# Spectral layer and MLP on one core: the fourth sequence's first stage as stacked products, and split loads in the passage to the MLP

## The chip, the cores and the metric

The kernel runs on one core of a Trainium2 chip. Its engines work side by side, each on its own queue in order: TensorE (PE, with its weight loads PEld), VectorE (DVE), ScalarE (ACT), GpSimd (POOL) and SyncE (SP), which here only starts transfers. Times are microseconds on the device, and the number that counts is the median of several runs.

## What is computed

Four sequences of 3008 tokens with 256 channels go through a spectral layer (a real Fourier transform over the tokens, a complex 256x256 product with bias, a soft threshold, the inverse transform) and then through an MLP with 2048 hidden channels.

```python
X = np.fft.rfft(x, axis=1)                       # x: (4, 3008, 256)
Yr = X.real @ w_r - X.imag @ w_i + b_r
Yi = X.real @ w_i + X.imag @ w_r + b_i
Yr, Yi = (np.sign(v) * np.maximum(np.abs(v) - 0.01, 0.0) for v in (Yr, Yi))
y = np.fft.irfft(Yr + 1j * Yi, n=3008, axis=1).reshape(12032, 256)
h = y @ moe_w_in                                 # 256 -> 2048
out = (h / (1 + np.exp(-h))) @ moe_w_out         # 2048 -> 256
```

## The kernel before

The transform is split as 3008 = 47 x 64. The first stage (`s1`) is a product over the 47, done for two halves of the 64 at once: 94 rows of x against a table with 96 columns, in eight pieces per sequence of 1024 columns each, one piece in two halves of 512. Its result goes through a scratch in DRAM. `s2_3` is the second forward stage, `mix3` the complex product, its deferred part the threshold, `split_z` and `i1` the first inverse stage, which stores into a second scratch; `i2` is the last inverse stage, which makes the columns `xt` of one block of 512 tokens for the MLP.

For precision, products of 32-bit numbers are made of high and low parts in a rounded 32-bit format (`F32R`): a value is cast on ScalarE, the difference is taken on VectorE, and three matmuls (high with high, high with low, low with high) stand for one. In the fourth sequence's first stage `s1_split` does the cast (L215) and the difference (L216) for one half, `s1_half` the three matmuls (L173) and the copy of the result (L226).

The order of the work is written by hand. After a prologue (the first sequence's spectral part, most of the second's first stage), the MLP runs in 384 ticks. Tick t does, in this order on every engine's queue: `split_g` of the tick before (L512, L513), the threshold left over from a mix product, `mlp1` of tick t (six matmuls at L495, then sigmoid and product on ScalarE and VectorE), the work that `fill` lists for tick t, a few stores, and `mlp2` of tick t - 2 (L535, L539). `put` finds for a piece of spectral work the next tick that is not in `taken`. The MLP weights come as 64-bit numbers and are turned into high and low parts in three steps of two VectorE instructions each, beside ScalarE casts; `w_go` does steps, and `W_GO` says how many in tick 0, 1, 2, and so on.

The passage from prologue to MLP stands at L734 to L755: the last two `u_step`, `s1` for pieces 2 to 5 of the second sequence, the loads of the first MLP block (`i2_load(0)`, two transfers at L409 of 96 rows from the second scratch), `i2` of block 0 with the two halves of piece 6 between (`s1_later`), the load for block 1. Piece 7 follows in the ticks.

Of the kernel before, what the change touches and what calls it, by code (L numbers as in the profile page):

```python
# [19 lines left out]
RR, KK = 47, 64  # L20
# [9 lines left out]
W_GO = [2, 1, 1, 2, 1, 1, 2, 1, 0, 0, 0, 2, 1, 2, 1, 2, 1, 2, 1, 1, 2, 1, 2, 1]  # L30

S1_SPLIT = (3, 4, 5, 6, 7)

# [4 lines left out]
def dft_tables():  # L38
# [16 lines left out]
    for h in range(2):  # L55
# [34 lines left out]
    c3f = c3  # L90
    return {
# [4 lines left out]
        "c3f": c3f,  # L96
    }
# [3 lines left out]
def spectral_mlp_kernel(ctx: ExitStack, tc: tile.TileContext, x, w_r, w_i, b_r, b_i, w_in, w_out, c1, c2, c3, c4, c3f, out):  # L101
# [9 lines left out]
    c4_sb = cst.tile([96, NP], F32, name="c4_sb")  # L111
    bias = cst.tile([128, 2, D], F32, name="bias")
# [48 lines left out]
    x_next = [(b, g) for b in range(NB) for g in range(8)]  # L161

    def x_ahead():
        if x_next:
            q = x_next.pop(0)
            x_t[q] = x_load(*q)
# [8 lines left out]
    def s1(b, g, late=False):  # L175
        t = x_t.pop((b, g))
        tag, bufs = ("s1o", 2) if 8 * b + g in (6, 7, 10, 11, 12, 13) else ("gin", 4)
        o = sb.tile([128, 4 * D], F32, tag=tag, bufs=bufs, name="s1o")[:96, :]
# [40 lines left out]
    def s1_half(b, g, i):  # L219
        sx = x_t.pop((b, g, i))  # L220
        if i == 0:
            x_t[b, g, "o"] = sb.tile([128, 4 * D], F32, tag="s1o", bufs=2, name="s1o")[:96, :]
        o = x_t[b, g, "o"]
        p = bank("s1")
        s1_product(p, (sx[:, 0, :], sx[:, 1, :]))
        nc.scalar.copy(o[:, i * 512:(i + 1) * 512], p[:96, :])  # L226
        if i == 0:
            s1_split(b, g, 1)
        else:
            v = scr1[b].rearrange("r (a j) d -> (r a) (j d)", a=4)  # L230
            store(v[:, g * 4 * D:(g + 1) * 4 * D], o)
            del x_t[b, g], x_t[b, g, "o"]
            x_ahead()

# [171 lines left out]
    def g_load(b, g):  # L406
        t = sb.tile([96, 4 * D], F32, tag="gin", bufs=4, name="gin")
        v = scr2[b].rearrange("r (a j) d -> (r a) (j d)", a=4)
        nc.sync.dma_start(out=t, in_=v[:, g * 4 * D:(g + 1) * 4 * D])  # L409
        g_t[b, g] = t  # L410
# [200 lines left out]
    with tc.manual_schedule():  # L611
# [123 lines left out]
        s1(1, 2, late=True)  # L735
        flush(1)
        u_step(NU + 1)
        s1(1, 3, late=True)
        i2_load(0)
        flush(1)  # L740
# [4 lines left out]
        flush(1)  # L745
# [40 lines left out]
        for i in range(2):  # L786
            put(2, s1_later, 7, i)
        for t in (11, 35):
            at(t, x_ahead)
        m3 = mix3_weights()  # L790
# [10 lines left out]
        for b, t0, dt in ((2, 37, 6), (3, 110, 8)):  # L801
# [49 lines left out]
```

## Time and profile before

| | us |
|---|---|
| median of 3 runs | 1383.81 (1381.85 to 1385.62) |
| profiled execution | 1383.51 |
| its span in the trace | 1381.5 |
| TensorE busy | 1363.3 |
| VectorE busy | 888.2 |
| ScalarE busy | 705.5 |
| GpSimd busy | 98.8 |

A group of instructions is named by the line of the kernel, the engine, the operation and the tiles it writes and reads. Matmuls overlap their neighbours, so the step from one start to the next is what one costs in a row. The granted clock (PEclk) is a share of TensorE's full 2.4 GHz; 0.50 is its lower level.

### The profile page before, as it was taken

The page shows a single profiled execution, that of the slowest core. Times are in us where ns is not written, and L with a number is a line of the kernel's source. Part 1 is how long each engine was busy: PE and PEld are TensorE (multiplying, and loading weights), DVE is VectorE, ACT ScalarE, POOL GpSimd, SP SyncE. Part 2 cuts the span into 40 slices and gives each one's busy share as a digit, 9 for nine tenths or more (in the row PEclk, how much of TensorE's full clock was granted, in tenths as well). Part 3 has the DMA queues.
Part 4 walks back from the last instruction along what each step waited for, and adds up shares of the span by engine and source line. Part 5 has one row for each costly group of instructions (what it writes and reads, how often), then busy time and mean ns, then how long its engine had stood idle before and what let it go on. Part 6 is the DMA issues. An engine that isn't in the chain of part 4 may idle for free.

```text
span 1381.5 us, 20358 instructions
## 1 busy us (share of the span) xinstructions
PE 1363.3 (99%) x7621; PEld 1168.3 (85%) x7621; DVE 888.2 (64%) x1517; ACT 705.5 (51%) x1386; POOL 98.8 (7%) x145
## 2 busy tenths in 40 slices
PE   8998999999999999999999999999999999999998
PEld 4976788888888888888888888888888888888888
DVE  3867979687655677767655577776654555455555
ACT  5445555555564555555454445454454444444444
POOL 2000012111000101111100011111000000000000
PEclk9999999999999999999999999999999999999999
DMA  8874334231423214333121022220210110011001
GB/s 263 268 226 144 93 88 119 76 97 32 123 76 101 58 43 107 89 94 81 50 73 54 20 77 60 75 81 25 61 32 12 27 39 10 18 27 39 0 16 24
DMA packets 69932, 103.51 MB, mean 75 GB/s; under 512 B 7306, under 2 KB 53002, under 8 KB 69834
## 3 DMA queue, kind: packets, MB, share of 16 engines
q1 hardware_dynamic: 58163, 79.07, 19.8%
q0 software_dynamic: 8096, 19.45, 5.4%
q10 hardware_dynamic: 3575, 3.70, 0.8%
q8 instruction: 60, 0.98, 0.3%
q14 instruction: 38, 0.31, 0.1%
HBM read 64.70 MB, written 37.49 MB: 74 GB/s over the span
## 4 chain that ended last, share of the span: by engine, by line
PE 94%; DMA 2%; DVE 2%; ACT 1%; issue 1%; SPq 0%; ACTq 0%; DVEq 0%
PE h L495 37%; PE acc L535 24%; PE acc L539 12%; PE mix L349 6%; PE i L438 3%; PE s L324 2%; PE mix L288 2%; PE s L173 2%; PE i L397 2%; PE s L189 1%; PE acc L530 1%; PE s L267 1%; PE i L394 1%; PE i2e L438 1%; DMA t3f<-in_c3f_dram 1%
## 5 line engine op out<-in xcount | busy, mean ns | idle before, releaser
L495 PE MATMUL h<-xt,win 128*128 128x512 f32 (+1 forms) x2304 | 585.5, 389 | 0.4 <-DVE g L503 0.2
L535 PE MATMUL acc<-wout,gh 128*128 128x512 f32 x1472 | 540.7, 401 | 0.0
L495 PEld LDWEIGHTS h<-xt,win 128*128 128x128 f32 x2304 | 401.7, 188 | 82.7 <-ACT xt L454 0.5
L502 ACT ACTIVATE g<-h 128x512 f32<-128x512 f32 (+1 forms) x385 | 226.1, 587 | 385.0 <-PE h L495 384.1
L503 DVE TENSOR_TENSOR g<-h,g 128x512 f32<-128x512 f32 (+1 forms) x385 | 261.0, 678 | 239.8 <-ACT g L502 236.5
L539 PE MATMUL acc<-wout,gl 128*128 128x256 f32 x1472 | 413.1, 281 | 1.3 <-DVE gl L513 1.3
L513 DVE TENSOR_TENSOR gl<-g,gh 128x512 fp32r<-128x512 f32 (+1 forms) x385 | 276.0, 717 | 169.2 <-ACT gh L512 165.0
L535 PEld LDWEIGHTS acc<-wout,gh 128*128 128x128 f32 x1472 | 277.6, 189 | 59.4 <-issue 0.5
L512 ACT CAST gh<-g 128x512 fp32r<-128x512 f32 (+1 forms) x385 | 235.3, 611 | 158.5 <-DVE g L503 155.9
L539 PEld LDWEIGHTS acc<-wout,gl 128*128 128x128 f32 x1472 | 278.6, 189 | 11.5 <-DVE gl L513 2.4
L356 POOL TENSOR_TENSOR q<-q,bias 128x256 f32<-128x256 f32 x36 | 26.4, 733 | 652.6 <-ACT q L355 652.6
L438 PEld LDWEIGHTS i<-c_sb,gin 96*128 96x128 f32 x420 | 54.9, 193 | 8.6 <-issue 4.3
L369 DVE TENSOR_TENSOR y<-q,mix 64x256 f32<-64x256 f32 x144 | 60.3, 419 | 2.2
L438 PE MATMUL i<-c_sb,gin 96*128 96x94 f32 x420 | 54.2, 274 | 3.3 <-DMA gin<-scr 3.3
L324 PEld LDWEIGHTS s<-t,a 128*128 128x128 f32 x288 | 37.7, 191 | 3.0
L324 PE MATMUL s<-t,a 128*128 128x128 f32 x288 | 37.9, 275 | 0.0
L455 DVE TENSOR_TENSOR xt<-i,xt 128x376 fp32r<-128x376 f32 (+2 forms) x48 | 28.0, 583 | 12.4 <-ACT xt L454 6.7
L173 PE MATMUL s<-sx,c 94*96 94x512 f32 (+1 forms) x111 | 34.1, 414 | 0.2 <-DVE sx L216 0.2
L397 PE MATMUL i<-zh,t 128*128 128x256 f32 x144 | 33.7, 297 | 0.0
L401 ACT COPY i1o<-i 128x512 f32<-128x512 f32 x48 | 27.8, 580 | 10.2 <-PE i L394 9.0
L556 DVE TENSOR_TENSOR o<-acc,o 128x256 f32<-128x256 f32 x92 | 32.6, 413 | 0.0
L357 POOL TENSOR_TENSOR q<-q,bias 128x256 f32<-128x256 f32 x36 | 31.9, 886 | 2.8
(118 smaller groups left out, 1164.7 us busy)
## 6 DMA issues: line engine op xcount, KB each, us to landing
a<-scr SPq DMA_DIRECT2D x48, 256.0 KB
gin<-scr SPq DMA_DIRECT2D x32, 384.0 KB
scr<-s1o SPq DMA_DIRECT2D x31, 384.0 KB
t<-in_c_dram POOLq DMA_DIRECT2D x36, 256.0 KB, 3.0
scr<-i1o SPq DMA_DIRECT2D x36, 256.0 KB
x_sb<-in_x_dram POOLq DMA_DIRECT2D x22, 376.0 KB, 4.1
t<-in_c_dram SPq DMA_DIRECT2D x48, 128.0 KB
w<-in_moe_w_in_dram SPq DMA_DIRECT2D x8, 512.0 KB
```

Source lines behind the costliest of these rows:

```text
L173: nc.tensor.matmul(out=p[:96, :], lhsT=c1_hl[m][:K, :], rhs=hl[k][:K, :], start=(n == 0), stop=(n == 2))
L324: nc.tensor.matmul(out=pv[:, e, :, r, :], lhsT=a[:, r, e * 128:(e + 1) * 128], rhs=t2[:, r * 128:(r + 1) * 128], start=True, stop=True,)
L349: nc.tensor.matmul(out=out, lhsT=x_[:, e, c, :], rhs=m[:, e, :], start=(n == 0), stop=(n == 5))
L397: nc.tensor.matmul(out=pv[:, r, :], lhsT=t3[:, m, q], rhs=z[k][:, r, :], start=(n == 0), stop=(n == 2),)
L438: nc.tensor.matmul(out=p[:, o:o + m], lhsT=g_t[b, j // 4][:, q:q + 128], rhs=c4_sb[:, p0:p0 + m], start=True, stop=True,)
L495: nc.tensor.matmul(out=p[:, :n], lhsT=w[:, e, f * 128:(f + 1) * 128], rhs=v[:, e, :n], start=(m == 0), stop=(m == 5),)
L502: nc.scalar.activation(out=g[:, q], in_=p[:, q], func=ACTF.Sigmoid)
L503: nc.vector.tensor_tensor(out=g[:, q], in0=p[:, q], in1=g[:, q], op=ALU.mult)
L512: nc.scalar.copy(gh[:, q], g[:, q])
L513: nc.vector.tensor_sub(gl[:, q], g[:, q], gh[:, q])
L535: nc.tensor.matmul(out=a, lhsT=gh[:, q], rhs=wout[:, f].rearrange("p a c -> p (a c)"), start=begins, stop=False,)
L539: nc.tensor.matmul(out=a[:, D:2 * D], lhsT=gl[:, q], rhs=wout[:, f, 0, :], start=False, stop=ends,)
```

## The change

Three things change.

The fourth sequence's first stage is done in sixteen pieces instead of eight, with the two halves of the 64 in separate pieces. A piece has 47 rows of x, and these are loaded twice, to rows 0 to 46 and 64 to 110 of one buffer; rows 32 to 63 are set to zero once for each of the two buffers. `stack_split` casts all 111 rows, and takes the difference in rows 64 to 110, so that high and low parts lie one above the other. The new table `c5` holds the table's high part in 48 columns and its low part in 48 others (from column 64), and both again for the lower rows. One matmul per 512 columns gives (high + low) times the high part in PSUM rows 0 to 47 and (high + low) times the low part in rows 64 to 111; these are copied out by ScalarE and added by VectorE.

In the passage the two loads of the first MLP block are each cut in two: 88 rows after the next to last inverse store, and the last 8 rows after the last one. The results of pieces 4 and 5 go to x buffers that are no longer in use, the two halves of piece 7 move to later ticks, and stores are started in another order.

`W_GO` has other numbers: 13 steps instead of 11 in ticks 0 to 7, and 17 instead of 19 from tick 11 on.

```diff
-W_GO = [2, 1, 1, 2, 1, 1, 2, 1, 0, 0, 0, 2, 1, 2, 1, 2, 1, 2, 1, 1, 2, 1, 2, 1]
+W_GO = [2, 2, 1, 2, 1, 2, 2, 1, 0, 0, 0, 2, 1, 2, 1, 2, 1, 2, 1, 2, 1, 1, 1]
+STACKED = 3
...
+    def x_load_twice(b, q):
+        t = x_sb[q % 2]
+        if b == STACKED and q < 2:
+            nc.gpsimd.memset(t[32:64, :], 0.0)
+        h, g = divmod(q, 8)
+        v = x[b].rearrange("(n h j) d -> n h (j d)", h=2, j=NJ)[:, h, g * 4 * D:(g + 1) * 4 * D]
+        for p in (0, 64):
+            nc.gpsimd.dma_start(out=t[p:p + RR, :], in_=v)
+        return t
...
-        tag, bufs = ("s1o", 2) if 8 * b + g in (6, 7, 10, 11, 12, 13) else ("gin", 4)
-        o = sb.tile([128, 4 * D], F32, tag=tag, bufs=bufs, name="s1o")[:96, :]
+        if b == 1 and g in (4, 5):
+            o = x_pre[g + 1][:96, :]
+        else:
+            tag, bufs = ("s1o", 2) if 8 * b + g in (6, 7, 10, 11) else ("gin", 4)
+            o = sb.tile([128, 4 * D], F32, tag=tag, bufs=bufs, name="s1o")[:96, :]
...
+    def stack_split(b, q):
+        t = x_t[b, q]
+        sx = sb.tile([128, 4 * D], F32R, tag="sx", bufs=1, name="sx")
+        nc.scalar.copy(sx[:64 + RR, :], t[:64 + RR, :])
+        nc.vector.tensor_sub(sx[64:64 + RR, :], t[64:64 + RR, :], sx[64:64 + RR, :])
+        x_t[b, q] = sx
+
+    def stack_product(b, q):
+        sx = x_t.pop((b, q))
+        o = sb.tile([128, 4 * D], F32, tag="s1o", bufs=2, name="s1o")[:2 * NR, :]
+        for i in range(2):
+            p = bank("s1")
+            c = slice(i * 512, (i + 1) * 512)
+            nc.tensor.matmul(out=p, lhsT=c5_sb[:64 + RR, :], rhs=sx[:64 + RR, c], start=True, stop=True)
+            nc.scalar.copy(o[:, c], p[64:64 + 2 * NR, :])
+            nc.vector.tensor_tensor(out=o[:, c], in0=p[:2 * NR, :], in1=o[:, c], op=ALU.add)
+        h, g = divmod(q, 8)
+        v = scr1[b].rearrange("r (i h j) d -> (r i) h (j d)", i=2, h=2)
+        store(v[:, h, g * 4 * D:(g + 1) * 4 * D], o)
+        x_ahead()
...
         u_step(NU)
         s1(1, 2, late=True)
+        for g in range(2):
+            loaded.add((0, g))
+            g_load(0, g, slice(0, 88))
         flush(1)
         u_step(NU + 1)
         s1(1, 3, late=True)
-        i2_load(0)
-        flush(1)
+        for g in range(2):
+            g_load(0, g, slice(88, 96))
         s1(1, 4, late=True)
         w_go()
         w_tags[:] = [(("zl", 2), ("zh", 2))]
         s1(1, 5, late=True)
-        flush(1)
+        flush(2)
...
-            put(2, s1_later, 7, i)
+            put(5, s1_later, 7, i)
...
+        at(30, nc.gpsimd.dma_start, c5_sb, c5)
...
-        for b, t0, dt in ((2, 37, 6), (3, 110, 8)):
+        t = 0
+        for q in range(16):
+            t = max(t, int(110 + 4.4 * q))
+            at(t, stack_split, 3, q)
+            t = put(t + 1, stack_product, 3, q)
+        for b, t0, dt in ((2, 37, 6),):
```

The changed kernel is longer, so its lines have other numbers: L409 becomes L461, L142 becomes L157, L579 becomes L630, L495, L535 and L539 become L546, L586 and L590, and L205 becomes L234.

On SyncE, in the passage, this stood in the row before: the store of piece 2 of the second sequence, the two loads of block 0, then stores and a weight load (`scr` with `s1o` is a store of the first stage, `gin` a block's load, `w` a weight load).

```order
L142 DMA scr_1_83<-s1o 96x1024
L409 DMA gin<-scr_0_86 96x1024 x2
L142 DMA scr_1_83<-s1o 96x1024
L579 DMA w_999<-in_moe_w_out_dram 128x2x512
L142 DMA scr_1_83<-s1o 96x1024
L409 DMA gin<-scr_0_86 96x1024
L142 DMA scr_1_83<-s1o 96x1024
L579 DMA w_1055<-in_moe_w_in_dram 128x1024
```

And now, at the same place on SyncE:

```order
L461 DMA gin<-scr_0_87 88x1024 x2
L157 DMA scr_1_84<-s1o 96x1024
L461 DMA gin<-scr_0_87 8x1024 x2
L630 DMA w_1000<-in_moe_w_out_dram 128x2x512
L157 DMA scr_1_84<-s1o 96x1024
L157 DMA scr_1_84<-x_pre 96x1024
L461 DMA gin<-scr_0_87 96x1024
L157 DMA scr_1_84<-x_pre 96x1024
L630 DMA w_1056<-in_moe_w_in_dram 128x1024
```

The long parts of the loads now stand ahead of the store of piece 2, the short parts behind it, and the stores of pieces 3 and 4 follow the weight load together.

On TensorE, tick 2 had the end of `mlp1`, the first half of piece 7 and the start of `mlp2` in this row before (`h` is `mlp1`, `s` the first stage, `acc` is `mlp2`):

```order
L495 MATMUL h<-xt_1013,win_79 128x512
L495 MATMUL h<-xt_1013,win_80 128x512
L495 MATMUL h<-xt_1014,win_79 128x512
L205 MATMUL s_1123<-x_sb_69,c_sb 96x512
L535 MATMUL acc<-wout,gh 128x512
L539 MATMUL acc<-wout,gl 128x256
```

And now, in tick 2 on TensorE:

```order
L546 MATMUL h<-xt_1014,win_80 128x512
L546 MATMUL h<-xt_1014,win_81 128x512
L546 MATMUL h<-xt_1015,win_80 128x512
L586 MATMUL acc<-wout,gh 128x512
L590 MATMUL acc<-wout,gl 128x256
```

The half of piece 7 is gone from here, and `mlp2` follows `mlp1` directly; the two halves stand in ticks 6 and 7.

On VectorE, ticks 132 and 133 (a step of the third sequence, then no spectral product) read like this before (`xs`, `xl` belong to the second stage, `zl` to the inverse, `g` and `gl` to the MLP):

```order
L334 TENSOR_TENSOR xs<-s_6008,xs 128x256
L336 TENSOR_TENSOR xl<-s_6008,xh 128x2x256
L337 TENSOR_TENSOR xl<-xs,xh 128x2x128
L383 TENSOR_TENSOR zl<-y,zh 128x512
L513 TENSOR_TENSOR gl<-g,gh 128x512
L503 TENSOR_TENSOR g<-h,g 128x512
L513 TENSOR_TENSOR gl<-g,gh 128x512
```

And now, in the same two ticks on VectorE:

```order
L384 TENSOR_TENSOR xs<-s_6033,xs 128x256
L386 TENSOR_TENSOR xl<-s_6033,xh 128x2x256
L387 TENSOR_TENSOR xl<-xs,xh 128x2x128
L433 TENSOR_TENSOR zl<-y,zh 128x512
L268 TENSOR_TENSOR sx<-x_sb_70,sx 47x1024
L564 TENSOR_TENSOR gl<-g,gh 128x512
L554 TENSOR_TENSOR g<-h,g 128x512
L279 TENSOR_TENSOR s1o<-s_6088,s1o 48x512
L279 TENSOR_TENSOR s1o<-s_6092,s1o 48x512
L564 TENSOR_TENSOR gl<-g,gh 128x512
```

The difference of a stacked piece now stands behind that step and ahead of the tick's `gl`, and the two additions of its product stand behind the next tick's `g`.

## Rows read from the trace of the kernel before

**Rows 1.** The page, busy time: engine, us, share of the span, instructions.
```profile
PE 1363.3 (99%) x7621; PEld 1168.3 (85%) x7621; DVE 888.2 (64%) x1517; ACT 705.5 (51%) x1386; POOL 98.8 (7%) x145
```

**Rows 2.** Waits of PE: line waited for, us in total, times, longest.
```profile
PE s L205 <- DMA x_sb<-in_x_dram: 3.7, 1, 3.7
```

**Rows 3.** Chain of waits, 88 to 120 us: start us, us, what.
```profile
90.62 2.89 DMA scr<-i1o
...
93.57 4.43 DMA gin<-scr
```

**Rows 4.** Stretches: us, then busy us (instructions) of each engine, clock, DMA share, GB/s.
```profile
core 0: us, PE busy (x) PEld busy (x) DVE busy (x) ACT busy (x) POOL busy (x), PEclk, DMA share, GB/s
28.00:34.00 6.00, 3.32 (x22) 2.36 (x21) 1.38 (x2) 2.61 (x6) 1.26 (x1) 1.00 0.73 218
95.00:98.00 3.00, 0.12 (x1) 0.00 (x0) 0.95 (x2) 0.12 (x1) 0.00 (x0) 1.00 0.92 254
98.00:104.00 6.00, 5.86 (x27) 4.30 (x28) 0.90 (x2) 2.78 (x7) 0.00 (x0) 0.72 0.54 211
114.00:120.00 6.00, 5.27 (x17) 4.06 (x18) 3.63 (x6) 2.37 (x5) 0.00 (x0) 0.72 0.28 90
104.00:130.00 26.00, 21.69 (x100) 16.67 (x99) 20.05 (x36) 13.31 (x27) 0.54 (x1) 0.93 0.56 164
```

**Rows 5.** Timeline of ACT, 86 to 92 us: start us, us, engine, line, operation, tiles.
```profile
87.93 0.37 ACTq L138 DMA_DIRECT2D scr<-i1o  x1
```

**Rows 6.** Timeline of DVE in the first ticks: g, then weight steps, then gl.
```profile
108.64 0.69 DVE L503 TENSOR_TENSOR g<-h,g 128x512 f32<-128x512 f32 x1 [0.58 <-ACT g L502]
109.25 0.68 DVE L608 TENSOR_TENSOR ww<-ww,wout 128x512 f32<-128x512 f32 x1
...
110.58 0.42 DVE L597 TENSOR_SCALAR ww<-ww 128x512 uint32<-128x512 uint32 x1
...
111.64 0.68 DVE L513 TENSOR_TENSOR gl<-g,gh 128x512 fp32r<-128x512 f32 x1
```

**Rows 7.** Timeline of tick 167 and the next tick's start: PE, then ACT's sigmoid.
```profile
714.06 1.55 PE L495 MATMUL h<-xt,win 128*128 128x512 f32 x6
715.45 0.86 PE L173 MATMUL s<-sx,c 94*96 94x512 f32 x3
716.14 0.40 PE L535 MATMUL acc<-wout,gh 128*128 128x512 f32 x1
...
717.54 1.55 PE L495 MATMUL h<-xt,win 128*128 128x512 f32 x6
...
715.71 0.60 ACT L502 ACTIVATE g<-h 128x512 f32<-128x512 f32 x1 [0.81 <-PE h L495]
```

**Rows 8.** Timeline of PE, 135.9 to 136.3 us: the first `mlp2` product of tick 8.
```profile
136.04 0.39 PE L535 MATMUL acc<-wout,gh 128*128 128x512 f32 x1
```

**Rows 9.** Timeline of all engines, 156 to 165 us: a later stop of PE.
```profile
158.58 3.01 POOL L312 TENSOR_TENSOR w32d<-w 128x512 f32<-128x512 f32 x2 [33.09 <-DMA bias<-in_b_i_dram]
...
158.67 1.78 DVE L608 TENSOR_TENSOR ww<-ww,win 128x512 f32<-128x512 f32 x1
...
162.79 0.39 PE L539 MATMUL acc<-wout,gl 128*128 128x256 f32 x1 [1.28 <-DVE gl L513]
```

**Rows 10.** Groups by line and shape: line, what, count | busy us, mean ns | idle before.
```profile
L216 DVE TENSOR_TENSOR sx<-x_sb,sx 94x512 fp32r<-94x512 f32 x32 | 22.4, 699 | 10.2 <-ACT sx L215 10.0
L215 ACT CAST sx<-x_sb 94x512 fp32r<-94x512 f32 x32 | 19.8, 618 | 0.0
L337 DVE TENSOR_TENSOR xl<-xs,xh 128x256 fp32r<-128x256 f32 x36 | 14.9, 415 | 0.0
L335 ACT CAST xh<-xs 128x256 fp32r<-128x256 f32 x36 | 14.6, 407 | 20.2 <-DVE xs L334 20.2
```

**Rows 11.** Timeline of tick 132: ACT's i1o, DVE's zl, PE after tick 133's `mlp1`.
```profile
591.20 0.57 ACT L401 COPY i1o<-i 128x512 f32<-128x512 f32 x1
...
591.33 0.69 DVE L383 TENSOR_TENSOR zl<-y,zh 128x512 fp32r<-128x512 f32 x1
...
592.33 0.40 PE L535 MATMUL acc<-wout,gh 128*128 128x512 f32 x1
```

More of the change, by code (lines that the diff above doesn't have):

```diff
@@ L90, in dft_tables @@
     c3f = c3
+    c, s = trig(np.outer(n2, r), RR)
+    c5 = np.zeros((128, 2, KK))
+    c5[:RR, 0, :2 * NR] = np.stack([c, -s], axis=2).reshape(RR, 2 * NR)
+    c5[:, :, 1] = 0.0
+    c5 = c5.astype(np.float32)
+    bits = c5[:RR, 0].view(np.uint32).astype(np.uint64)
+    c5h = ((bits + 0x7FF + ((bits >> 12) & 1)) & 0xFFFFF000).astype(np.uint32).view(np.float32)
+    c5[:RR, 1] = c5[:RR, 0] - c5h
+    c5[:RR, 0] = c5h
+    c5[64:64 + RR] = c5[:RR]
     return {
@@ L96, in dft_tables, with spectral_mlp_kernel @@
         "c3f": c3f,
+        "c5": c5.reshape(128, 128),
     }
 @with_exitstack
-def spectral_mlp_kernel(ctx: ExitStack, tc: tile.TileContext, x, w_r, w_i, b_r, b_i, w_in, w_out, c1, c2, c3, c4, c3f, out):
+def spectral_mlp_kernel(ctx: ExitStack, tc: tile.TileContext, x, w_r, w_i, b_r, b_i, w_in, w_out, c1, c2, c3, c4, c3f, c5, out):
     nc = tc.nc
@@ L111, in spectral_mlp_kernel @@
     c4_sb = cst.tile([96, NP], F32, name="c4_sb")
+    c5_sb = cst.tile([128, 128], F32R, name="c5_sb")
     bias = cst.tile([128, 2, D], F32, name="bias")
@@ L159, in x_load @@
         return t
-    x_next = [(b, g) for b in range(NB) for g in range(8)]
+    def x_load_twice(b, q):
[7 more added lines that the diff above has]
+        return t
+    x_next = [(b, g) for b in range(NB) for g in range(16 if b >= STACKED else 8)]
     def x_ahead():
@@ L165, in x_ahead @@
             q = x_next.pop(0)
-            x_t[q] = x_load(*q)
+            x_t[q] = (x_load_twice if q[0] >= STACKED else x_load)(*q)
     x_t = {}
@@ L404, in spectral_mlp_kernel, with g_load @@
     g_t = {}
-    def g_load(b, g):
-        t = sb.tile([96, 4 * D], F32, tag="gin", bufs=4, name="gin")
+    def g_load(b, g, rows=slice(0, 96)):
+        if (b, g) not in g_t:
+            g_t[b, g] = sb.tile([96, 4 * D], F32, tag="gin", bufs=4, name="gin")
         v = scr2[b].rearrange("r (a j) d -> (r a) (j d)", a=4)
-        nc.sync.dma_start(out=t, in_=v[:, g * 4 * D:(g + 1) * 4 * D])
-        g_t[b, g] = t
+        nc.sync.dma_start(out=g_t[b, g][rows, :], in_=v[rows, g * 4 * D:(g + 1) * 4 * D])
     def pieces(c0, n):
```

## Prediction, made before the changed kernel was timed

> **What bounds the kernel now.** I read the page first: TensorE is busy for 1363.3 of the 1381.5 us span [rows 1], so nearly everything else is cover, and only two things can move the end: matmuls taken off TensorE, and stretches in which it waits or runs at its lower clock. Next I read who waited for whom and the chain of waits. One wait stands out, 3.7 us for a late piece of x in front of line 205 [rows 2]. The other is the passage from the spectral part to the MLP: the last store of the first inverse stage leaves at 90.62 and takes 2.89 us, the load of its result leaves at 93.57 and takes 4.43 [rows 3], and TensorE is busy for 0.12 of the 3 us from 95 to 98 [rows 4]. The table of stretches gives a second price of these two stops: after each of them the granted clock is 0.72 on the mean of the next 6 us, which is a time at the lower level of 1.2 GHz [rows 4]. A loss of 0.28 x 6 = 1.7 us each. The weaker pauses at 28 to 34 us, where TensorE is busy for 3.32 of 6 us, were not followed by a lower clock in that stretch, which shows 1.00 [rows 4]. What the two stops cost is then 3.0 + 1.7 + 3.7 + 1.7 = 10.1 us, and the first stage of the fourth sequence (48 matmuls at line 173 in sixteen ticks) is the third place that the change touches.
>
> **The change part by part.** *The split loads.* Before, both loads of the first MLP block wait for the last store, which lands at 90.62 + 2.89 = 93.5 [rows 3]. Now 88 of the 96 rows wait only for the store before it, which is issued at 87.93 [rows 5]; at the same 2.89 us it has landed by 90.8, and at 4.43 us the long parts are in by 95.3. Eight rows of each load still wait for 93.5. The trace has no load of 32 KB: it costs more than nothing, and less than the 4.43 us of a full one. I take the 2.89 us of the 256 KB store, the nearest transfer with a row, since the traffic around it is alike: 93.6 + 2.9 = 96.5, against 98.14 before [rows 3] (93.57 + 4.43 and a short start). Bounds are 93.6 and 98.0, so a gain of 0.1 to 3.0, and 1.6 taken. The Trainium skill (DMA: Bandwidth & Descriptors, section "Anatomy of one DMA — SWDGE (gpsimd) path") gives a transfer about 2.0 us that do not shrink with its size; an estimate from that page, which fits another kind of queue, would put the short loads at 95.6 and the sum 0.9 us lower. No row here shows a load so short. Four load issues instead of two stand on SyncE, and the store of an s1 result is moved behind the long ones; its queue has nothing urgent there, and ScalarE no longer waits for this store to release an output buffer, since the results of pieces 4 and 5 go to idle x buffers. One wait is added by that: the low part of xt for block 1 lies in the buffer from which piece 5 is stored. That store stands behind the third load of the MLP, at about 101 us; at 4.4 us it lands by 105.5, and VectorE comes to that xt after a product and three weight steps at about 109. It costs nothing; were the store late, the weight steps and splits queued behind on VectorE would be too. The stop of TensorE shrinks from 3.0 to about 1.4 us. As a stop of that weight was not followed by the lower clock [rows 4], I count the 1.7 us too: 3.3 us by the start of the first MLP products.
>
> *The late piece of x.* The two matmuls of line 205 for piece 7 move from ticks 2 and 4 to ticks 6 and 7 (5 is taken), some 10 us later, and the piece lands long before. That wait of 3.7 us and the 1.7 us of clock go, but VectorE is what comes next: during this stop it worked on, and in 104 to 130 us it has 20.05 us of work in 26 [rows 4]. The table of weight steps also puts 12 of them instead of 10 into ticks 0 to 6. From [rows 6], a step costs 1.33 us (two instructions, 109.25 to 110.58) or 1.06 (110.58 to 111.64), 1.2 on the mean, and a product or a split of g 0.61 (108.64 to 109.25). The products of tick 8 need the split of f = 6. VectorE's work from its first g to there: 12 x 1.2 + 14 x 0.61 + 1.5 (my allowance for four short instructions on xt) = 24.4 us, from 108.64 - 3.3 = 105.3, so 129.7. TensorE's floor is lower: it could start tick 2 at 106.0, and six ticks of 2.79 us (717.54 - 714.06 less the product's 0.69 [rows 7]) and 3 us, a wide allowance, for the i2 and s1 matmuls among them take it to tick 8 at 125.7, and to its second products at 127.1. So about 2.6 us of waiting for VectorE take the place of the wait removed. Before, those products begin at 136.04 [rows 8]. The gain at that point is 136.0 - 129.7 = 6.3 us, in which the 3.3 of the loads is contained. I take 6.4 for the passage, with 3.3 (VectorE returns all of the second stop) and 10 (it returns nothing) as ends.
>
> *The rest of the weight steps.* One stop of 1.28 us comes later [rows 9], behind a VectorE step of 1.78 us that is 0.69 in [rows 6], beside 3.01 us of POOL arithmetic. Fewer steps are left for these ticks, so that by their number alone it could vanish and the sum would be 1.3 us lower. The Trainium skill (GPSIMD Engine Reference, section "Specifications") says that POOL shares its SBUF interface with VectorE and contends with instructions that have two SBUF inputs; by that the stop belongs to the POOL work, and the trace agrees with 1.78 beside 0.69. POOL's work stays, so I leave the stop in.
>
> *The fourth sequence's first stage.* Sixteen products of three matmuls, 0.69 us each [rows 7] (715.45 to 716.14), become sixteen of two: 16 x 0.23 = 3.7 us off TensorE. That is bought with wider work: the cast on ScalarE is 1024 columns instead of 512, the subtraction on VectorE too, and one PSUM copy becomes two copies and two additions. From [rows 10], 256 columns more cost 0.21 us on ScalarE and 0.28 on VectorE, so the wide cast is 0.62 + 0.42 = 1.04 and the subtraction 0.70 + 0.57 = 1.27 (ends: as 512, or twice, 1.24 and 1.40). Both must be done before the first matmul, whereas before the first two needed less. What hides them is the time between the split's tick and the product's. In six of the sixteen the product stands in the very next tick with no mix product to lengthen the first. Worst are ticks 127 and 132, where the split stands behind a whole step of the third sequence. In tick 132 [rows 11] ScalarE is through with i1o at about 591.7 (copies overlap by 0.1), VectorE with zl at 592.0. Cast to 592.7, subtraction to 594.0; TensorE is free at 592.33: 1.6 us lost, twice, 3.3. In the four lighter ones (158, 162, 167, 171) the sum goes as in tick 167 [rows 7]: tick from 714.06, sigmoid until 716.2, cast to 717.3, subtraction to 718.5, that is 4.5 us, where TensorE, without the product that stands there today, is ready after 2.79 + 1.39 = 4.2. About 0.3 each, 1.2 in all. The other ten have a mix product or a whole tick between and cost nothing; their cover is gone if VectorE falls more than about 1.4 us behind. Loading x twice, the two memsets and the new table lie on POOL and queues with time to spare. The stage gives 3.3 + 1.2 - 3.7 = +0.8 us; ends -3.7 and, with cast and subtraction at their upper ends (0.33 us more in each of the six ticks), +2.8.
>
> Sum: -6.4 + 0.8 = -5.6 us. The profiled execution took 1383.51 us (span 1381.5 and 2.0 around it), the median of the runs is 1383.81; both lose 5.6, so the median becomes 1378.2.
>
> **The rivals.** *The stage pays.* If the wide cast and subtraction cost hardly more than the narrow ones (0.99 us less in the chain of each tick), 0.65 us remain of each of the two worst stalls, nothing of the small ones: 1.3 - 3.7 = -2.4, with -6.4 gives -8.8, 1375.0. For it: the copies are mostly idle-covered. Against: the durations in [rows 10] grow with the columns.
> *VectorE returns the second stop.* Its queue is in order, so each weight step put forward delays the next g; if ticks 2 to 8 run at its pace, only the 3.3 us of the loads stay: -3.3 + 0.8 = -2.5, 1381.3. For it: 20.05 us of work in a stretch that is to become 6 us shorter [rows 4]. Against: 6 us of idle in that same row.
> *The split loads do not run ahead.* If the long parts are held on SyncE until 93.5 after all (each also waits for the release of a weight buffer), 6.4 - 3.3 = 3.1 remain: -2.3, 1381.5.
> *Slower.* VectorE has some 1.9 us more per piece (1.27 - 0.70, and two additions of about 0.7) in the stage, and what it owes is handed on to the next tick. If it is 1.4 us behind on entering the split ticks, all nine products that follow their split in the next tick lose 1.6 us: 14.4 - 3.7 - 6.4 = +4.3, 1388.1. It decides from the point where the subtraction ends 1.6 us after TensorE has come to the product, as in tick 132, in the ticks with a mix product too. Against: idle on VectorE around the split ticks.
>
> **How the numbers follow.** Forecast 0.58, its own range 1375.5 to 1380.0 from the ends above; the stage pays 0.17; VectorE returns it 0.15; loads not ahead 0.05; slower 0.05. A measurement of this kernel tells 0.3%, 4.15 us, from no change: faster means below 1379.7. Of the forecast 0.55 lies below: 0.55 + 0.17 = 0.72 faster. The rest of it and the two weak cases, 0.23, are within. Slower 0.05. The range runs from 1373.0 (the second stop returned by nothing and a stage that pays in part) to 1382.0, over the two weak cases; it leaves out the slow case and tails of some 0.12.
>
> **What would show it.** The profile after should have the first i2 matmul at about 96.5, no 3.7 us wait at s1_later, a clock of 1.00 through 98 to 104 and no run of 0.5, waits for gl in ticks 2 to 8, the 1.3 us stop still there near 150 to 155, and 32 matmuls of the stage with waits for sx at only a few products. A long gin wait, a clock at 0.5 in the passage, or sx waits in most products would make it wrong.

## The result, and the profile after

The change made the kernel slower: 1393.01 us median of 6 runs (1391.52 to 1394.56) against 1382.96 us before (6 runs, 1379.77 to 1389.14), a ratio of 1.0071 with a 95% interval of 1.0056 to 1.0086. The profiled execution took 1394.56 us, its span is 1392.8. The forecast was 1378.2.

The page's busy times, the answer to [rows 1] (engine, us, share of the span, instructions), and then the waits of TensorE, the answer to [rows 2] (line waited for, us in total, times, longest):

```profile
PE 1363.6 (98%) x7605; PEld 1164.4 (84%) x7605; DVE 914.9 (66%) x1549; ACT 718.5 (52%) x1402; POOL 111.3 (8%) x172
```

```profile
PE i L489 <- DMA gin<-scr: 5.8, 2, 4.8
PE s L277 <- DVE sx L268: 3.9, 4, 1.6
PE s L277 <- DVE y L419: 3.9, 3, 1.3
PE acc L590 <- DVE gl L564: 3.4, 6, 1.6
```

TensorE has 16 matmuls less, but its busy time is no shorter (1363.6 us against 1363.3), and its share of the span falls from 99% to 98%. The wait for x at `s1_later` is gone from the list. In its place stand four others: the loads of the first two MLP blocks cost 5.8 us, 4.8 of them for the first (3.3 and 3.0 before), the products of the new stage wait for their subtraction (line 268) and, unforeseen, for the threshold (line 419), and `mlp2` waits for `gl` six times where it was once.

In the passage, the chain of waits of after (start us, us, what) and the issues on SyncE there:

```profile
92.32 7.16 DMA scr<-i1o
99.48 0.02 issue
99.50 1.98 DMA gin<-scr
```

```profile
91.84 0.72 SPq L461 DMA_DIRECT2D gin<-scr  x2
92.66 0.31 SPq L157 DMA_DIRECT2D scr<-s1o  x1
99.50 0.60 SPq L461 DMA_DIRECT2D gin<-scr  x2
```

The last store of the first inverse stage takes 7.16 us from issue to landing; it took 2.89 [rows 3]. Half a microsecond ahead of it stand the two long loads. The short loads behind it take only 1.98.

The table of stretches, the answer to [rows 4]:

```profile
core 0: us, PE busy (x) PEld busy (x) DVE busy (x) ACT busy (x) POOL busy (x), PEclk, DMA share, GB/s
95.00:98.00 3.00, 1.82 (x5) 0.43 (x3) 1.38 (x2) 2.63 (x5) 0.00 (x0) 1.00 0.73 239
98.00:104.00 6.00, 2.39 (x11) 2.42 (x12) 0.00 (x0) 0.00 (x0) 0.00 (x0) 0.63 0.51 157
104.00:114.00 10.00, 9.03 (x41) 6.15 (x40) 5.08 (x10) 5.12 (x11) 0.00 (x0) 0.88 0.65 198
114.00:120.00 6.00, 5.12 (x29) 4.06 (x27) 5.90 (x11) 3.09 (x6) 0.00 (x0) 1.00 0.53 137
```

The first stop of TensorE is longer than before (2.39 us of work in 98 to 104) and is followed by the lower clock (0.63, then 0.88). The second, in 114 to 120, is gone with its clock, 1.00 instead of 0.72. By these rows the lower level takes 0.37 x 6 + 0.12 x 10 = 3.4 us from the passage, against 0.28 x 6 = 1.7 us behind the first stop before.

The new stage's operations, by line and shape (count | busy us, mean ns | idle before), against [rows 10]:

```profile
L267 ACT CAST sx<-x_sb 111x1024 fp32r<-111x1024 f32 x16 | 16.8, 1049 | 0.0
L268 DVE TENSOR_TENSOR sx<-x_sb,sx 47x1024 fp32r<-47x1024 f32 x16 | 21.6, 1352 | 7.8 <-ACT sx L267 7.6
L279 DVE TENSOR_TENSOR s1o<-s,s1o 48x512 f32<-48x512 f32 x32 | 20.4, 675 | 0.0
```

For the comparisons below, three lengths are read from each trace. A tick starts with its first `mlp1` matmul; the executions differ by up to 2.7 us in when the first `s2` product starts (at 28.7 to 31.4 us), so that lengths inside a trace tell more than its end does. *Store* is from the issue of the last i1o store to that of the load that waits for it; *tick 24* is counted from the same issue; *ticks 2 to 24* is the stretch of the weight steps, *100 to 182* that of the fourth sequence's first stage.

| kernel | store | tick 24 | ticks 2 to 24 | 100 to 182 | median |
|---|---|---|---|---|---|
| before | 2.95 | 90.4 | 71.65 | 293.60 | 1382.96 |
| after | 7.18 | 93.0 | 71.76 | 300.08 | 1393.01 |
| e1_passage | 7.33 | 93.3 | 71.75 | 293.58 | 1386.52 |
| e2_stage | 2.95 | 88.0 | 69.20 | 300.14 | 1388.86 |
| e3_whole_loads | 2.93 | 90.3 | 71.76 | 300.12 | 1391.32 |
| e4_gap | 7.15 | 93.3 | 71.70 | 291.12 | 1385.87 |
| e5_later_alone | 2.96 | 86.5 | 67.76 | 293.62 | 1379.73 |
| e6_one_long | 5.45 | 92.0 | 71.74 | 300.07 | 1391.21 |
| e7_early_weights | 2.94 | 88.3 | 69.48 | 291.03 | 1380.54 |
| e8_stage_gap | 2.95 | 90.6 | 70.86 | 291.04 | 1380.21 |
| e9_old_table | 7.25 | 88.6 | 67.96 | 300.07 | 1388.93 |
| e10_later_gap | 2.96 | 87.6 | 67.82 | 291.13 | 1376.63 |
| e11_early | 3.12 | 87.2 | 66.28 | 291.07 | 1378.41 |
| e12_pairing | 2.95 | 90.4 | 71.95 | 293.58 | 1384.63 |

Stretches that are alike in two kernels agree to 0.2 us. Only where the late piece of x is waited for (before, e2, e8) does the length of ticks 2 to 24 vary, 69.2 to 71.7 us. What varies is the wait, 3.7 us before, 2.7 in e2 and 2.9 in e8, and the clock behind it, which fell in the kernel before [rows 4] and in e8, but not in e2 (e2 first, then e8):

```profile
PE s L231 <- DMA x_sb<-in_x_dram: 2.7, 1, 2.7
114.00:120.00 6.00, 4.99 (x27) 4.04 (x28) 5.14 (x10) 3.69 (x7) 0.00 (x0) 1.00 0.32 94
```

```profile
PE s L231 <- DMA x_sb<-in_x_dram: 2.9, 1, 2.9
114.00:120.00 6.00, 5.90 (x23) 4.31 (x23) 3.75 (x6) 2.13 (x5) 0.00 (x0) 0.72 0.30 90
```

Without the wait and the 0.28 x 6 = 1.7 us of clock the three have 66.3, 66.5 and 66.3 us.

### The profile page after: what moved, and what is told of

The parts are those of the page before. It is cut to its first block, busy times and chain, and to the rows that moved or that the text cites. A ratio compares the mean times of both kernels' runs of the same rounds, so it can differ in the third digit from the quotient of the medians.

```text
span 1392.8 us, 20467 instructions
## 1 busy us (share of the span) xinstructions
PE 1363.6 (98%) x7605; PEld 1164.4 (84%) x7605; DVE 914.9 (66%) x1549; ACT 718.5 (52%) x1402; POOL 111.3 (8%) x172
## 4 chain that ended last, share of the span: by engine, by line
PE 88%; DMA 4%; DVE 4%; ACT 3%; issue 2%; SPq 0%; DVEq 0%; ACTq 0%
PE h L546 35%; PE acc L586 23%; PE acc L590 12%; PE mix L399 5%; PE i L489 3%; PE s L374 2%; PE i L447 2%; DMA scr<-i1o 1%; PE mix L338 1%; DMA scr<-s1o 1%; PE acc L581 1%; PE s L199 1%; DVE gl L564 1%; PE i2e L489 1%; PE s L277 1%
## 5 line engine op out<-in xcount | busy, mean ns | idle before, releaser
L546 PE MATMUL h<-xt,win 128*128 128x512 f32 (+1 forms) x2304 | 584.9, 389 | 0.0
L586 PE MATMUL acc<-wout,gh 128*128 128x512 f32 x1472 | 540.4, 401 | 0.7 <-ACT gh L563 0.7
L546 PEld LDWEIGHTS h<-xt,win 128*128 128x128 f32 x2304 | 400.9, 188 | 82.2 <-DVE xt L506 0.4
L590 PE MATMUL acc<-wout,gl 128*128 128x256 f32 x1472 | 412.8, 280 | 3.5 <-DVE gl L564 3.4
L586 PEld LDWEIGHTS acc<-wout,gh 128*128 128x128 f32 x1472 | 276.9, 188 | 61.0 <-ACT gh L563 2.4
L590 PEld LDWEIGHTS acc<-wout,gl 128*128 128x128 f32 x1472 | 278.0, 189 | 15.4 <-DVE gl L564 6.2
L505 ACT CAST xt<-i 128x376 fp32r<-128x376 f32 (+2 forms) x48 | 24.2, 503 | 19.6 <-PE i L489 19.6
```

Source lines behind the costliest of these rows:

```text
L546: nc.tensor.matmul(out=p[:, :n], lhsT=w[:, e, f * 128:(f + 1) * 128], rhs=v[:, e, :n], start=(m == 0), stop=(m == 5),)
L586: nc.tensor.matmul(out=a, lhsT=gh[:, q], rhs=wout[:, f].rearrange("p a c -> p (a c)"), start=begins, stop=False,)
L590: nc.tensor.matmul(out=a[:, D:2 * D], lhsT=gl[:, q], rhs=wout[:, f, 0, :], start=False, stop=ends,)
```

## The experiments

### The two parts, each alone

The passage alone is the changed kernel with the first stage of before:

```diff
-        t = 0
-        for q in range(16):
-            ...
-        for b, t0, dt in ((2, 37, 6),):
+        for b, t0, dt in ((2, 37, 6), (3, 110, 8)):
```

> The passage part of the change alone: split loads, pieces 4 and 5 in x buffers, line 234 later, new table of weight steps; the first stage of the fourth sequence as before. Theory: the profiled loss is the sum of two separate losses, 4.3 us in the passage (up to tick 24) and 6.4 in the stage. Then this kernel is 4.3 us slower than before, about 1387.3, its last i1o store takes some 7 us instead of 2.9, TensorE stops for about 5 us before the first i2 product, and after tick 24 no tick is later or earlier by over 0.5. Rival: the long store of the profiled execution was an accident, and the passage gains as forecast: 1377.

Measured: 1386.52, ratio 1.0022 (1.0011 to 1.0033). The store takes 7.31 us here too:

```profile
89.54 7.31 DMA scr<-i1o
96.87 1.91 DMA gin<-scr
```

It was no accident, and the passage costs instead of paying. The other half is the kernel before with the new stage:

> The first stage of the fourth sequence alone (x loaded twice, one product for both parts), the passage as before. Theory: 6.4 us slower than before, about 1389.4: 5.1 us in six waits for the subtraction, 4.4 in three waits of a second product for its PSUM bank (line 419 behind the subtraction on VectorE), about 1 in small gaps around the products, 3.7 saved; tick 0 at 104 us as before. Rival: the waits of the stage come from a VectorE that is already behind out of the passage; without the new passage they shrink, and the stage is between -1 and +2: 1382 to 1385.

Measured: 1388.86, ratio 1.0044 (1.0029 to 1.0059); ticks 100 to 182 are 6.5 us longer, as in the changed kernel, and TensorE has the same two waits (in this kernel, lines 265 and 416):

```profile
PE s L274 <- DVE sx L265: 3.9, 4, 1.6
PE s L274 <- DVE y L416: 3.9, 3, 1.3
```

So the parts do not touch each other: the stage's loss is its own, and the rival, a VectorE that comes late out of the passage, is out.

### What held the store

```diff
-        for g in range(2):
-            loaded.add((0, g))
-            g_load(0, g, slice(0, 88))
         flush(1)
         u_step(NU + 1)
         s1(1, 3, late=True)
-        for g in range(2):
-            g_load(0, g, slice(88, 96))
+        i2_load(0)
```

> The changed kernel with the two first loads of the MLP whole again and issued behind the last i1o store, as before; all else as changed. Theory: the long loads, issued 0.5 us ahead of that store, held it up (7.1 us instead of 2.9). Then the store lands within 3.6 us of its issue, tick 0 starts at 104 to 105, and the time falls by some 4 us to about 1389. Rival: the store is slow for the other traffic of that moment (the s1 result stored right behind it, weights), and takes 6 us or more here too: no change, 1393, or more, since the loads then start last.

The store is back at 2.87 us, by the chain of this kernel:

```profile
88.99 2.87 DMA scr<-i1o
...
92.34 4.75 DMA gin<-scr
```

The mechanism held; the size did not. Tick 24 comes 2.7 us earlier behind the store's issue, not 4, because the split has its own gain, a short load of 1.98 us in place of a whole one of 4.75. The median, 1391.32 (1388.45 to 1392.19 in 4 runs), lies between the two expectations, and its ratio to before, 1.0066 (1.0046 to 1.0086), cannot be told from the 1.0071 of the changed kernel; that the store held the passage up is read from the lengths inside the traces. The dose of it was tried with one long load ahead instead of two:

```diff
-        for g in range(2):
-            loaded.add((0, g))
-            g_load(0, g, slice(0, 88))
+        loaded.add((0, 0))
+        g_load(0, 0, slice(0, 88))
```

> The changed kernel with only one of the two long loads (88 rows of piece 0) issued ahead of the last i1o store; the load of piece 1 is whole again and behind it. Theory: the store shares the transfer engines with what was issued just ahead of it, so half the bytes ahead cost about half of the 4.2 us: it lands some 5 us after its issue, and the time is 1391 to 1393. Rival: what holds the store up is the s1 result issued 0.3 us behind it, which is here too: 7 us again.

```profile
90.47 5.43 DMA scr<-i1o
```

None, one and two loads of 352 KB ahead give 2.87, 5.43 and 7.16 us. The s1 result on SyncE is issued within 0.4 us of that store in the last two alike; with none ahead it is issued 1.0 us earlier. What moved between the store's issue and its landing, with none, one and two loads ahead:

```profile
DMA packets 366, 0.58 MB, mean 203 GB/s; under 512 B 32, under 2 KB 288, under 8 KB 366
DMA packets 483, 1.02 MB, mean 187 GB/s; under 512 B 43, under 2 KB 299, under 8 KB 483
DMA packets 582, 1.38 MB, mean 192 GB/s; under 512 B 54, under 2 KB 310, under 8 KB 582
```

The rate is nearly the same; what grows is the amount. The store is 0.26 MB of each. The rest is SyncE's queue, with 0.32, 0.75 and 1.11 MB: the s1 result (0.39 MB) is in all three, whole in the last two and with 0.32 MB in the first, so that of the first step at most 0.07 MB, some 0.4 us at this rate by an estimate, can be its; the rest of both steps is the long loads. The median is 1391.21, as expected, tick 24 only 1.0 earlier than in the changed kernel.

The Trainium skill (DMA: Bandwidth & Descriptors, section "Queues, rings and completion order") says that a transfer engine goes round the queues for which it has work, a packet from each. By that a store on ScalarE's queue isn't behind SyncE's loads but beside them; this trace agrees: in the changed kernel 85 of the 272 packets on the store's queue run from 92.3 to 95.0 us, none from 95.0 to 96.5 and the others after that, with SyncE's packets in all three stretches.

### A tick between split and product

```diff
-            t = put(t + 1, stack_product, 3, q)
+            t = put(t + 2, stack_product, 3, q)
```

> The changed kernel with one whole tick more between each piece's split and its product (the product at least two ticks behind instead of one). Theory: the waits for the subtraction (5.1 us) go, and most of the waits for the PSUM bank too, since line 419 no longer stands behind a subtraction of 1.7 us: 8 to 9 us less than the changed kernel, about 1384.5. Rival: VectorE as a whole has too much to do between ticks 110 and 180, so the waits move from sx and the bank to gl: 1391 to 1393.

Measured: 1385.87, ratio 1.0027 (1.0015 to 1.0038), so 7.1 below the changed kernel (some 6 by the two ratios). Ticks 100 to 182 went from 300.08 to 291.12 us: 9.0, and 2.5 below the 293.60 of before. Of the waits in the stage this is left:

```profile
PE s L277 <- DVE y L419: 0.3, 1, 0.3
```

The rival, waits that move to `gl`, is out. Two causes were expected to go with this one edit, and the trace of after shows both of them. First the subtraction, in tick 128:

```profile
580.40 1.22 DVE L268 TENSOR_TENSOR sx<-x_sb,sx 47x1024 fp32r<-47x1024 f32 x1 [0.73 <-ACT sx L267]
```

```profile
581.77 0.47 PE L277 MATMUL s<-sx,c_sb 111*128 111x512 f32 x1 [1.62 <-DVE sx L268]
```

And then the second half of a product behind a mix tick, VectorE and TensorE from 509 us:

```profile
509.00 1.74 DVE L268 TENSOR_TENSOR sx<-x_sb,sx 47x1024 fp32r<-47x1024 f32 x1 [0.79 <-ACT sx L267]
510.78 0.69 DVE L564 TENSOR_TENSOR gl<-g,gh 128x512 fp32r<-128x512 f32 x1
511.48 1.72 DVE L419 TENSOR_TENSOR y<-q,mix 64x256 f32<-64x256 f32 x4
```

```profile
511.65 0.40 PE L277 MATMUL s<-sx,c_sb 111*128 111x512 f32 x1
513.35 0.47 PE L277 MATMUL s<-sx,c_sb 111*128 111x512 f32 x1 [1.30 <-DVE y L419]
```

The first half starts at 511.65, the second only at 513.35, when line 419 has read the mix product. Both come from `bank`, which has two PSUM banks in the ticks; a stacked product needs both, and one of them still holds the mix product until the threshold has read it, and that stands on VectorE behind the wide subtraction. The next experiment puts the same stage into the kernel before:

> The kernel before with the new first stage of the fourth sequence, its products two ticks behind their splits; the passage as before. Theory: the stage gives 2.5 us (ticks 100 to 182 in 291.1 us instead of 293.6, as in the changed kernel with that gap) and nothing else changes: 1380.2. Rival: the later products cost something at the end (the changed kernel with the gap had 1.7 us more behind its last tick): 1382.

Measured: 1380.21, ratio 0.9987 (0.9976 to 0.9998), with 291.04 us in the stage. The stage's gain is there at its forecast size; by the ratio the kernel is 0.3 to 3.3 us faster. Behind the start of its last tick e8 has 8.3 us, e4 9.0, e7 (below) 9.4, the changed kernel 7.9 and the one before 7.4; what makes these up to 2 us was not followed.

### The late piece of x alone

```diff
-            put(2, s1_later, 7, i)
+            put(5, s1_later, 7, i)
```

By now the theory was that VectorE gives back all of the 5.4 us, as ticks 2 to 24 were no shorter in the changed kernel (71.76) than in the one before (71.65):

> The kernel before with one edit: the two s1_later matmuls of piece 7 in ticks 6 and 7 instead of 2 and 4. Theory: VectorE's work sets the end of ticks 2 to 22 (58 of 66 us busy before), so the wait of 3.7 us for x goes and comes back as waits for gl: tick 24 lies 88 to 90.4 us behind the issue of the last i1o store, as in the two runs with the old passage, and the time is within 1 us of before, about 1382.6. Rival (the prediction's step): only 2.6 of 5.4 us come back, tick 24 at 86 to 87.6, 1380.

Measured: 1379.73, ratio 0.998 (0.997 to 0.9989), ticks 2 to 24 in 67.76 us. The theory fell. This one edit on the kernel before saves 3.9 us in that stretch: the wait of 3.7 us and the 1.7 us of lower clock behind it are gone, and 1.5 come back.

```profile
98.00:104.00 6.00, 4.78 (x26) 3.11 (x24) 0.89 (x2) 2.96 (x7) 0.00 (x0) 1.00 0.65 206
104.00:114.00 10.00, 7.47 (x35) 5.73 (x36) 8.60 (x16) 6.01 (x11) 0.00 (x0) 1.00 0.57 188
114.00:120.00 6.00, 6.00 (x35) 5.21 (x34) 5.86 (x11) 2.31 (x5) 0.00 (x0) 1.00 0.56 175
```

The 1.00 in 98 to 104 us, where the kernel before has 0.72, cannot come from the edit, which comes later in the run; the passage is the one of before. But it shows what that lower clock cost. Tick 2 starts 18.7 us behind the issue of the last i1o store here and 18.8 before: the first products of `mlp1` wait for `xt` and `g` instead (0.84, 1.03 and 0.77 us). In e8 and e10, with the same passage and 3.4 us lost to the lower level there (0.81 in 95 to 98 us and 0.53 in 98 to 104 in e8), tick 2 starts at 19.7.

In the changed kernel, then, something else in the passage part takes 4 us between ticks 2 and 24. A run made beside it, the changed kernel with whole loads and the gap, still followed the fallen theory and put VectorE's work forward, into its idle time ahead of the first xt (with one step less in tick 0):

```diff
-        w_go()
+        w_go(2)
         i2(0, 0)
+        w_go()
         s1_later(6, 0)
         i2_ends(0)
+        w_go()
         s1_later(6, 1)
         i2(0, 1)
-        w_go()
         i2_load(1)
         flush(2)
-        w_go()
```

> The changed kernel with whole loads behind the last store, the gap of two ticks in the stage, and three weight steps put forward into the time in which VectorE is idle before the first i2 and xt (it is idle for 9 us there in the run with whole loads), one step less in tick 0. Theory (VectorE's work from the first g to tick 22 is the bound): about 3 us of that work leave the bound stretch, tick 24 lies some 87 us behind the issue of the last i1o store, the stage gives 2.5: 1377 to 1378. Rival: ticks 16 to 22 wait for the arithmetic on POOL and not for the amount of VectorE's work; then ticks 5 to 15 come earlier but tick 24 does not: 1380.

It has 69.48 us for ticks 2 to 24, 2.3 less than the changed kernel, where 1.7 more were still to be had by e5; tick 24 comes at 88.3 and not at 87, and the time is the rival's, 1380.54, ratio 0.9983 (0.9972 to 0.9994). Ticks 15, 17 and 18 are long (3.33, 5.33, 4.27 us against 2.79, 4.32 and 2.78 in e5), far behind the ticks that were relieved. Tick 18 ran in part at the lower clock (0.50 in 158 to 160 us, 0.69 in 160 to 162). The other two pointed to the table of weight steps, which is the new one here.

### The table of weight steps

A weight takes three steps in turn: VectorE writes `ww` (lines 648, 649); ScalarE casts it (line 652) while VectorE takes the exponents (655, 656); VectorE makes the low part (659, 660). From tick 11 to tick 18 both tables call 2, 1, 2, 1 steps; but the new one has called two more before, so other steps fall together.

```diff
-W_GO = [2, 2, 1, 2, 1, 2, 2, 1, 0, 0, 0, 2, 1, 2, 1, 2, 1, 2, 1, 2, 1, 1, 1]
+W_GO = [2, 1, 1, 2, 1, 1, 2, 1, 0, 0, 0, 2, 1, 2, 1, 2, 1, 2, 1, 1, 2, 1, 2, 1]
```

> The changed kernel with one edit: the table of weight steps of before. Theory: the new table shifts the phase of the weight steps, so that from tick 11 on the step that writes ww (line 649) and the one whose cast on ScalarE reads it (line 652) are called in the same tick; ScalarE then waits for VectorE with the tick's gh and sigmoid behind it. With the old table these stand in different ticks: ticks 2 to 24 take 67.8 us instead of 71.8, as in the run with line 205 alone moved, and the time is 4 us below the changed kernel, 1389. Rival: the table does nothing, and what the changed passage lost lies in the stores and output buffers it moved: 1393, ticks 2 to 24 in 71.8 us.

Measured: 1388.93, ratio 1.0035 (1.0023 to 1.0047), ticks 2 to 24 in 67.96 us: 3.8 less by the table alone. By ticks, the changed kernel is longer in ticks 15, 17, 19 and 21 (by 0.6, 0.9, 0.8 and 0.5 us) and in tick 8 (by 0.8); ticks 2 to 7 together differ by 0.1. ScalarE's waits for line 649 in the ticks, first in the changed kernel (110 to 180 us), then with the old table (109 to 175):

```profile
ACT wout L652 <- DVE ww L649: 11.8, 6, 2.5
ACT win L652 <- DVE ww L649: 4.9, 2, 2.5
```

```profile
ACT wout L652 <- DVE ww L649: 2.7, 2, 1.8
ACT win L652 <- DVE ww L649: 2.6, 1, 2.6
```

16.7 us in eight waits against 5.3 in three. What one of them does, in the changed kernel on ScalarE and on VectorE from 160 us:

```profile
161.89 0.62 ACT L652 CAST win<-ww 128x512 fp32r<-128x512 f32 x1 [2.47 <-DVE ww L649]
162.41 0.67 ACT L646 ACTIVATE ww<-w 128x512 f32<-128x512 f32 x1
162.99 0.60 ACT L563 CAST gh<-g 128x512 fp32r<-128x512 f32 x1
163.49 0.59 ACT L553 ACTIVATE g<-h 128x512 f32<-128x512 f32 x1
```

```profile
160.11 0.69 DVE L554 TENSOR_TENSOR g<-h,g 128x512 f32<-128x512 f32 x1
160.71 0.42 DVE L648 TENSOR_SCALAR ww<-ww 128x512 uint32<-128x512 uint32 x1
161.16 0.69 DVE L649 SCALAR_TENSOR_TENSOR ww<-w,ww 128x512 uint32<-128x512 uint32 x1
```

`g` is ready at 160.8, and ScalarE, which had been idle for 2.47 us, casts it only at 162.99: ScalarE stood in front of line 652, which waits for line 649, and `gh` is behind that in its queue. Line 564 and `mlp2` follow late. Ahead of tick 8 it is the same pair, which the new table's second step in tick 6 puts together: ScalarE waits 2.38 us in front of line 652, until 134.58, and `gh`, whose `g` is ready at 133.5, comes at 136.15. To tell the pairing from the mere number of steps, the same pairing was put into e5, with one step less ahead of tick 7:

```diff
-W_GO = [2, 1, 1, 2, 1, 1, 2, 1, 0, 0, 0, 2, 1, 2, 1, 2, 1, 2, 1, 1, 2, 1, 2, 1]
+W_GO = [2, 1, 1, 2, 1, 1, 1, 1, 0, 0, 0, 2, 1, 2, 1, 2, 1, 2, 1, 2, 1, 2, 1, 2]
```

> The kernel of e5_later_alone with one weight step less in tick 6, and the steps from tick 11 on in the same numbers but with that step late, so that, as with the new table, lines 598 and 601 of a weight fall into one tick. Fewer steps lie ahead of ticks 7 to 16 than in e5. Theory (the pairing costs): ticks 15, 17, 19 and 21 are 0.5 to 0.9 us longer each, ticks 2 to 24 take 69.5 to 70.5 us, 1382. Rival (what costs is the number of steps put forward): no more than e5's 67.8 us, 1379.5 or less.

Measured: 1384.63, ratio 1.0011 (1.0 to 1.0021); ticks 2 to 24 take 71.95 us, 4.2 more than in e5, even more than expected. ScalarE's waits are back (105 to 176 us):

```profile
ACT wout L601 <- DVE ww L598: 9.4, 5, 2.5
ACT win L601 <- DVE ww L598: 7.5, 3, 2.6
```

That is 16.9 us in eight waits, against 6.5 in four in e5. With fewer steps early on it is slow, so it isn't their number: from tick 11 to 18 the two tables have the same numbers, and ticks 15 and 17 are 0.6 and 0.9 us longer than in e5. Tick 8 takes the same in both (2.8 us), so that e12 does not test the 0.8 us there.

### What pays, put together

Line 205's move (e5) and the stage with the gap (e8), in the kernel before, with nothing else of the change:

> The kernel before with what paid: the two matmuls of piece 7 in ticks 6 and 7, and the new first stage of the fourth sequence with its products two ticks behind the splits; loads, output buffers and the table of weight steps as before. Theory: the two gains lie in different stretches and add up, 3.5 + 2.5 = 6.0 us: 1377.2. Rival: each median carries over 1 us of scatter and one of the two is smaller than it looked: 1379 to 1380.

Measured: 1376.63, ratio 0.9954 (0.9935 to 0.9972), 16.4 us below the changed kernel and faster than both. The two gains add up: 6.4 us by the ratio (3.9 to 9.0, from 4 runs), where 6.0 were expected, and in the trace 3.8 in ticks 2 to 24 and 2.5 in ticks 100 to 182. The page's line of it:

```profile
PE 1359.8 (99%) x7605; PEld 1164.5 (85%) x7605; DVE 913.6 (66%) x1549; ACT 718.1 (52%) x1402; POOL 110.8 (8%) x172
```

On top of it, weight steps put forward with the old phase kept:

> The kernel of e10_later_gap with two weight steps put forward into VectorE's idle time ahead of the first xt and a third before the first tick, and one step less in tick 0, so that the phase from tick 1 on is that of the old table. Theory: some 1 to 2 us of VectorE's work leave ticks 2 to 8, where it is waited for: tick 24 at 85 us behind the issue of the last i1o store, 1375.5. Rival: ScalarE, which waits for the weights' load in the second of these steps, holds up the casts behind it: 1377 or more.

Ticks 2 to 24 take 66.28 us, 1.5 less. But tick 1 is 5.08 us long instead of 3.16, waiting for the load of block 1, and tick 24 comes only 0.4 earlier:

```profile
PE i L486 <- DMA gin<-scr: 2.6, 1, 2.6
```

Its median, 1378.41 with a ratio of 0.9968 (0.995 to 0.9985), cannot be told from that of e10. The time is in the rival's range, but what TensorE waits for is the load and not a cast on ScalarE. What made that load late wasn't followed up.

## Why the prediction was wrong

It forecast -6.4 for the passage and +0.8 for the stage, and +10.05 was measured; each alone, the passage has +3.0 (e1) and the stage +6.1 (e2) by the ratios. By the stretches: the store +2.7 (after against e3), the table +3.8 (after against e9), line 205 -3.9 (e5 against before; against e2 and e8, which wait less for x, and e2 without the lower clock, 1.4 and 3.1), the stage +6.5: +9.1, within the interval of 7.7 to 11.9 that the ratio gives.

**The split loads: the failed step is "Eight rows of each load still wait for 93.5".** That is the last store landing after the 2.89 us it took before. The sum has the first i2 5.9 us behind that store's issue (96.5 - 90.62); it started 9.3 behind it (7.5 before), since the store took 7.16. The prediction priced each load by the traffic around *it* and never asked what 704 KB just ahead would do to the store that everything waits for. It even had the rival "do not run ahead"; they did run ahead, and that was the fault. The gain of 3.3 became a loss of 2.7. The short load, on the other hand, was dearer in the sum than it is: 1.98 us against the 2.89 taken. For it the Trainium skill (DMA: Bandwidth & Descriptors, section "Anatomy of one DMA — SWDGE (gpsimd) path") has about 2.0 us for another kind of queue, and 1.98 lies close to that.

The 3.3 also held 1.7 us of clock, and that term was too large: e5 loses none at the lower level behind the first stop, and the kernel before 1.7. Tick 0 then starts 1.0 us sooner, but the `g` from which the sum counts VectorE's work (108.64 [rows 6]) stands 18.0 us behind the store's issue in both, and tick 2 starts no sooner. In the changed kernel the stop did not shrink, so its clock did not come back; it lost 3.4. Of the 2.7 some 0.6 may be that: e9, with the same loads and store but 1.7 lost, starts tick 2 at 20.6 us behind the store's issue, the changed kernel at 21.2, e3 (1.7 too) at 18.5. Why one and the same passage loses 0, 1.7 or 3.4 us to the clock stays open.

**The late piece of x: right, and better than forecast.** In the changed kernel the `mlp2` products of tick 8 [rows 8] begin 23.25 us behind the start of tick 2, in the one before 26.65: 3.4 us gained. The sum has 129.7 - 106.0 = 23.7 for this stretch, 3.0 gained. So of the 5.4 us of the second stop 2.0 came back with twelve weight steps there (1.5 with ten, in e5).

**The weight steps: the failed step is counting them.** Twelve steps at 1.2 us were added to VectorE's queue. That ScalarE takes part in each weight, in order, with `gh` and the sigmoid behind it, stood nowhere in the sum; neither did the ticks from 11 to 18, where the numbers in the two tables are the same and only the phase differs. Of the 3.8 us 2.8 were lost in ticks 15 to 21 and 0.8 in tick 8, next to nothing in ticks 2 to 7. The rival "VectorE returns the second stop" foresaw that this gain could be lost again, but from VectorE's amount of work, which e5 and e12 rule out. The 1.3 us stop stayed, as said, and grew: tick 17 takes 5.26 us instead of 4.34, with the new pairing only.

**The stage: prices right, one wait missed.** The cast was put at 1.04 us and took 1.05, the subtraction at 1.27 and took 1.22 where nothing lies beside it. The waits for it were put at 4.5 us and came to 5.1: 1.8 twice, in ticks 128 and 133, and 0.2 to 0.6 in four, the very ones. The failed step is "The other ten have a mix product or a whole tick between and cost nothing". Three with a mix product ahead (pieces 0, 1 and 9) waited 1.5 us each for a PSUM bank, 4.4 in all. The prediction counted the tick's time for the subtraction and did not look at the two banks, which a product of two halves needs at once. There were 0.2 more in piece 2 and 1.0 in small gaps around the products, where the kernel before had 0.6: 5.1 + 4.6 + 1.0 - 0.6 - 3.7 = 6.4, against 6.5 measured. The rival "slower" named the nine products that did wait, these three and the six, but its +4.3 is right in sign only: it holds +10.7 for the stage and keeps -6.4 for the passage. Its mechanism, a VectorE debt handed on from tick to tick, did not show: the stage alone lost the same.

## What to carry to other kernels

Before a transfer is put ahead of another, ask who waits for the other one: a large load that may start early can slow a store that must land early, though they are on different queues. A table that only says how many steps a tick gets also says which steps meet in it; when one engine's step feeds another engine within a tick, shifting the phase by one puts a wait in front of everything else in that engine's queue. And a product that is made shorter on TensorE by wider work elsewhere needs its distance from that work set anew, counted in ticks and in PSUM banks: the same edit cost 6.5 us at a distance of one tick and gave 2.5 at two.

## What the runs showed of the hardware

A store of 256 KB took 2.87 us, 5.43 with one load of 352 KB issued ahead of it from another engine's queue, and 7.16 with two; all that moved in these times went at 203, 187 and 192 GB/s. A load of eight rows (32 KB) took 1.98 and 1.91 us, where whole ones took 4.4 to 4.8. The same subtraction on VectorE (47x1024) took 1.22 us in twelve pieces of the changed kernel and 1.74 to 1.75 in the four (0, 1, 9 and 10) where POOL's addition of line 407 runs beside its first 0.7 us; in e4 piece 1 stands two ticks later, without POOL, and took 1.22. The Trainium skill (GPSIMD Engine Reference, section "Specifications") has the two engines share an interface to SBUF, which agrees.
